# Loading a gated MLP's weights with four adjacent rows per partition instead of one

## The chip, the cores and the metric

One NeuronCore of a Trainium2 chip runs the kernel. The metric is device time in microseconds (us) of one execution; lower is better. The span that the profile of one execution shows is about 2 us shorter than the device time of that execution (62.4 and 64.23 us). Executions of one kernel here spread by about 1.5%. A run that is over 1.5% above the fastest of its kernel is called slow and left out of every ratio below; the others are the "fast" runs.

## The reference

```python
B, S, D, F = 32, 1, 1024, 3584          # all bfloat16
def reference(x, W_gate, W_up, W_down):
    gate = jnp.einsum("bsd,df->bsf", x, W_gate)      # 32x1024 @ 1024x3584
    up   = jnp.einsum("bsd,df->bsf", x, W_up)
    gate = gate * (gate > 0)                         # ReLU
    return jnp.einsum("bsf,fd->bsd", gate * up, W_down)   # 32x3584 @ 3584x1024
```

There are 32 rows of x and 22 MB of weights, each used once. That is a weight-streaming problem.

## The kernel before

All weight loads are issued by SP, ahead of everything, into SBUF that holds all three matrices. Each load has its own semaphore.

```python
Wg_sb = [P, KT, F];  Wu_sb = [P, KT, F];  Wd_sb = [P, NJT, D]      # P = 128, KT = 8, NJT = 28
for k in range(KT):                        # 16 transfers, each partition gets ONE row: 7168 bytes
    dma_list.append((("wg", k), Wg_sb[:, k, :], W_gate[k * P : (k + 1) * P, :]))
    dma_list.append((("wu", k), Wu_sb[:, k, :], W_up[k * P : (k + 1) * P, :]))
for n, gsz in enumerate([4, 4, 4, 4, 4, 4, 2, 1, 1]):   # 9 transfers, rows j*128 + p: 2048 bytes each
    dma_list.append((("wd", n), Wd_sb[:, j0:j1, :],
                     W_down[j0 * P : j1 * P, :].rearrange("(j p) d -> p j d", p=P)))
# ... cut ...
@block.sync
def _(sp):
    sp.dma_start(x_sb[:, :], x2).then_inc(sem_x, 16)
    for key, dst, src in dma_list:
        sp.dma_start(dst, src).then_inc(dma_sem[key], 16)
    issue_out_dmas(sp, "sp")               # output pieces go out on SP, ACT, POOL, SP
```

PE transposes x, then multiplies each weight tile as it lands, with x as the stationary operand, four 32-row results side by side in PSUM. ACT applies the ReLU, DVE multiplies by `up`, PE transposes the result (`h`), and W_down's tiles are multiplied as they land. The kernel waits for the last W_down tile, adds it, copies the sum out of PSUM and stores it in four pieces.

## Time and profile before

| | before |
|---|---|
| device time, median of 3 runs | 64.21 us (63.45 to 64.31) |
| span of the profiled execution | 62.4 us |
| PE busy | 25.6 us (41%) |
| HBM read | 22.09 MB, 355 GB/s over the whole span |

The page's slices of the span come first. Each column is a fortieth of the span (1.56 us). Digits are the busy share in tenths; "DMA" is the mean of the 16 DMA engines, "GB/s" what they moved.

```profile
PE   0202463265246326524632060293780533517800
...
DMA  0699999999999999999999999999999999993000
GB/s 0 180 400 405 414 423 423 428 432 428 423 418 428 418 418 418 428 414 423 414 418 424 414 410 381 386 389 386 385 390 385 389 386 386 389 385 139 11 20 22
```

The DMA row is 9 from the third slice to the thirty-sixth while PE is half idle: the stream of weights is the bound. The GB/s row has two plateaus, about 420 (gate and up) and about 387 (W_down). The windows view gives them exactly. Its columns are the window and its length, the busy time of each engine, the recorded PE clock, the DMA share and GB/s.

```profile
6.00:37.00 31.00, 14.51 (x98) 1.81 (x97) 0.00 (x0) 0.00 (x0) 0.00 (x0) 1.00 1.01 421
44.00:54.00 10.00, 4.80 (x76) 2.30 (x80) 0.69 (x1) 0.83 (x2) 0.00 (x0) 1.00 1.05 387
```

The chain that ended last, as the page sums it:

```profile
SPq L134 75%; DMA Wd_sb<-in_W_down_dram 16%; POOL out_dram L124 1%; PE O_ps L254 1%; ACT o_sb L168 1%; SPq L132 1%
```

"SPq L134" is the line that issues the weights. Its first twelve issues take 0.4 to 0.8 us each and later ones up to 9.2 us, while earlier transfers are still under way. What holds the later ones the trace does not show; with the DMA row at 9 throughout we count their time as the stream's. So read, 91% of the chain is the stream, and what follows it is short. The costliest group of the last stage, with its idle time, says the same from PE's side (7.7 us busy, 7.8 us idle before its instructions, of which W_down transfers ended 7.1):

```profile
L254 PE MATMUL O_ps<-Wd_sb,hT_sb 128*32 128x256 bf16 x112 | 7.7, 413 | 7.8 <-DMA Wd_sb<-in_W_down_dram 7.1
```

The trace also records every DMA packet and every semaphore increment. Each of these transfers raises its semaphore 16 times, and the page counts 16 DMA engines; the trace names no engine, and we read one landing as one engine. That fits the pace of gate and up: 128 packets of 7168 bytes are 8 for each engine, at 272 ns 2.18 us, and from the third transfer on their 8th landings come 2.17 to 2.20 us apart. These are the landings of four transfers, in us from the start of the span; "8th" is about the median engine:

```
before              8th     15th    16th
W_up, k=5          29.37   29.93   29.93
W_up, k=6          33.74   34.31   35.78
W_up, k=7          38.10   38.69   40.03
W_down, last piece 57.05   57.59   58.85
```

From 33.6 us on one engine is 1.2 to 1.5 us behind the fifteen others, and the last matmuls wait for it (they start at 58.90 us, the last landing is at 58.85). At 33.60 us the trace has a 16384-byte packet of the queue named "instruction", 1.07 us long; after that name we call it an instruction fetch.

### The profile page before, as it was taken

To read this page: it belongs to the slowest core of one execution; us is meant where nothing else is said; L and a number is where in the kernel's file an instruction comes from. 1 tells how busy PE (TensorE), PEld (TensorE's weight loads), DVE (VectorE), ACT (ScalarE), POOL (GpSimd) and SP (SyncE) were. 2 spreads that over 40 slices of the span, in tenths; PEclk is the share of its full clock that TensorE was granted. 3 is DMA by queue.
4 is the path that set the end of the run, shared out by engine and by line. 5 is a ranking of instruction groups with operands and counts; after the bars stand their busy time and mean duration, and the time that the engine had idled before them with its cause. 6 is when DMAs were issued, how large, how long until landed. Compare 5 with 4: busy or idle time off the path is not lost.

```text
span 62.4 us, 560 instructions
## 1 busy us (share of the span) xinstructions
PE 25.6 (41%) x240; PEld 6.6 (11%) x240; DVE 1.4 (2%) x2; ACT 4.2 (7%) x7; POOL 1.3 (2%) x7
## 2 busy tenths in 40 slices
PE   0202463265246326524632060293780533517800
PEld 0101000000000000000000000122340220303100
DVE  0000000000000000000000000013400000000000
ACT  5320000000000000000000000032430000000020
POOL 4000000000000000000000000000000000000030
DMA  0699999999999999999999999999999999993000
GB/s 0 180 400 405 414 423 423 428 432 428 423 418 428 418 418 418 428 414 423 414 418 424 414 410 381 386 389 386 385 390 385 389 386 386 389 385 139 11 20 22
DMA packets 6258, 22.19 MB, mean 356 GB/s; under 512 B 480, under 2 KB 592, under 8 KB 6256
## 3 DMA queue, kind: packets, MB, share of 16 engines
q1 hardware_dynamic: 6176, 22.12, 89.9%
q8 instruction: 2, 0.03, 0.2%
q10 hardware_dynamic: 48, 0.02, 0.1%
q0 software_dynamic: 32, 0.02, 0.1%
HBM read 22.09 MB, written 0.07 MB: 355 GB/s over the span
## 4 chain that ended last, share of the span: by engine, by line
SPq 75%; DMA 16%; issue 2%; POOL 1%; PE 1%; ACT 1%
SPq L134 75%; DMA Wd_sb<-in_W_down_dram 16%; POOL out_dram L124 1%; PE O_ps L254 1%; ACT o_sb L168 1%; SPq L132 1%
## 5 line engine op out<-in xcount | busy, mean ns | idle before, releaser
L201 PE MATMUL G_ps<-Wg_sb,xT_sb 128*32 128x512 bf16 x56 | 8.6, 618 | 13.0 <-DMA Wg_sb<-in_W_gate_dram 9.7
L201 PE MATMUL U_ps<-Wu_sb,xT_sb 128*32 128x512 bf16 x56 | 8.6, 621 | 9.5 <-DMA Wu_sb<-in_W_up_dram 9.5
L254 PE MATMUL O_ps<-Wd_sb,hT_sb 128*32 128x256 bf16 x112 | 7.7, 413 | 7.8 <-DMA Wd_sb<-in_W_down_dram 7.1
L254 PEld LDWEIGHTS O_ps<-Wd_sb,hT_sb 128*32 128x32 bf16 x112 | 3.2, 125 | 11.9 <-DMA Wd_sb<-in_W_down_dram 8.0
L159 ACT ACTIVATE g_sb<-G_ps 128x512 bf16<-128x512 f32 (+1 forms) x2 | 1.2, 596 | 37.8 <-PE U_ps L201 37.8
L201 PEld LDWEIGHTS G_ps<-Wg_sb,xT_sb 128*32 128x32 bf16 x56 | 1.3, 108 | 19.6 <-DMA Wg_sb<-in_W_gate_dram 12.3
L201 PEld LDWEIGHTS U_ps<-Wu_sb,xT_sb 128*32 128x32 bf16 x56 | 1.3, 109 | 16.1 <-DMA Wu_sb<-in_W_up_dram 15.9
L176 DVE TENSOR_TENSOR h_sb<-U_ps,g_sb 128x512 bf16<-128x512 f32 (+1 forms) x2 | 1.4, 690 | 43.7 <-ACT g_sb L159 43.7
L124 POOL DMA_DIRECT2D out_dram<-o_sb x1 | 0.6, 621 | 58.5 <-ACT o_sb L168 58.5
L188 PE MATMUL HTB_ps<-ident,x_sb 32*128 32x32 bf16 x8 | 0.4, 186 | 2.6 <-DMA x_sb<-in_x_dram 2.6
L155 ACT ACT_TABLE_LOAD x1 | 1.3, 1283 | 0.7 <-PEq L285 0.7
L168 ACT CAST o_sb<-O_ps 128x256 bf16<-128x256 f32 x1 | 0.4, 372 | 13.2 <-PE O_ps L254 13.2
L232 PE MATMUL HTA_ps<-ident,h_sb 128*128 128x128 bf16 x4 | 0.6, 308 | 0.6 <-DVE h_sb L176 0.6
L163 ACT COPY hT_sb<-HTA_ps 128x512 bf16<-128x512 bf16 x1 | 0.6, 586 | 1.4 <-PE HTA_ps L232 1.4
L232 PE MATMUL HTB_ps<-ident,h_sb 96*128 96x96 bf16 x4 | 0.5, 276 | 0.2 <-DVE h_sb L176 0.2
L163 ACT COPY hT_sb<-HTB_ps 128x384 bf16<-128x384 bf16 x1 | 0.5, 478 | 1.3 <-PE HTB_ps L232 1.3
L188 PEld LDWEIGHTS HTB_ps<-ident,x_sb 32*128 32x128 bf16 x8 | 0.3, 101 | 2.6 <-DMA x_sb<-in_x_dram 2.6
L232 PEld LDWEIGHTS HTA_ps<-ident,h_sb 128*128 128x128 bf16 x4 | 0.3, 130 | 1.5 <-DVE h_sb L176 1.5
L155 ACT COPY xT_sb<-HTB_ps 128x256 bf16<-128x256 bf16 x1 | 0.4, 372 | 1.0 <-PE HTB_ps L188 1.0
L232 PEld LDWEIGHTS HTB_ps<-ident,h_sb 96*128 96x128 bf16 x4 | 0.3, 127 | 0.7 <-DVE h_sb L176 0.7
L141 POOL TENSOR_SCALAR_AFFINE_SELECT ident<-ident 128x128 bf16<-128x128 bf16 x1 | 0.3, 287 | 0.2 <-POOL ident L139 0.2
L139 POOL MEMSET ident<- 128x128 bf16 x1 | 0.2, 204 | 0.3 <-POOLq L285 0.3
(4 smaller groups left out, 0.4 us busy)
## 6 DMA issues: line engine op xcount, KB each, us to landing
Wg_sb<-in_W_gate_dram SPq DMA_DIRECT2D x8, 896.0 KB, 16.1
Wu_sb<-in_W_up_dram SPq DMA_DIRECT2D x8, 896.0 KB, 17.8
Wd_sb<-in_W_down_dram SPq DMA_DIRECT2D x6, 1024.0 KB, 18.0
Wd_sb<-in_W_down_dram SPq DMA_DIRECT2D x1, 512.0 KB, 14.7
Wd_sb<-in_W_down_dram SPq DMA_DIRECT2D x2, 256.0 KB, 10.4
x_sb<-in_x_dram SPq DMA_DIRECT2D x1, 64.0 KB, 1.8
out_dram<-o_sb SPq DMA_DIRECT2D x2, 16.0 KB, 1.5
out_dram<-o_sb ACTq DMA_DIRECT2D x1, 16.0 KB, 1.6
```

Of the source, the lines that this page charges most:

```text
L124: eng.dma_start(dst, src).then_inc(sem_out[i], 16)
L132: sp.dma_start(x_sb[:, :], x2).then_inc(sem_x, 16)
L134: sp.dma_start(dst, src).then_inc(dma_sem[key], 16)
L155: act.copy(out=xT_sb[:, :], in_=xT_ps).then_inc(sem_xT_sb, 1)
L159: act.activation(out=g_sb[g][0:np_, :], in_=G_ps[g][0:np_, :], func=ACT.Relu).then_inc(sem_g, 1)
L163: act.copy(out=hT_sb[g][:, :, 0:np_], in_=HT_ps[g].rearrange("p (t q) -> p t q", t=TPC)[:, :, 0:np_],).then_inc(sem_hT_sb, 1)
L168: act.copy(out=o_sb[:, :], in_=O_ps[:, 0:DQ]).then_inc(sem_o, 1)
L176: dve.tensor_tensor(out=h_sb[g][0:np_, :], in0=U_ps[g][0:np_, :], in1=g_sb[g][0:np_, :], op=ALU.mult,).then_inc(sem_h, 1)
L188: ins = pe.transpose(xT_ps[:, k * NB : (k + 1) * NB], x_sb[:, k * P : (k + 1) * P], ident[0:NB, 0:NB],)
L201: return pe.matmul(ps[q * NB : (q + 1) * NB, :], lhsT=xT_sb[:, k * NB : (k + 1) * NB], rhs=w[:, k, c * FC : (c + 1) * FC], start=(k == 0), ...
L232: ins = pe.transpose(HT_ps[g][:, t * P : t * P + np_], h_sb[g][0:np_, t * P : (t + 1) * P], ident[0:np_, 0:np_],)
L254: ins = pe.matmul(O_ps[q * NB : (q + 1) * NB, 0:DQ], lhsT=hT_sb[g][:, t, qq * NB : (qq + 1) * NB], rhs=Wd_sb[:, j, q * DQ : (q + 1) * DQ], ...
```

## The change

The intent: give each partition several rows that are adjacent in HBM and adjacent in SBUF, so that a DMA packet is longer. The row order inside a contraction is free, provided that x (or h) is transposed in the same order; so the transposes read every fourth column. The waits become coarser: 4 gate/up transfers instead of 16. POOL issues no output piece any more: the third piece moves from POOL to SP and the fourth from SP to ACT. The core of the diff:

```diff
-WD_GROUPS = os.environ.get("GLU_WDG", "4,4,4,4,4,4,2,1,1")
+BLOCKS = [4, 4]  # rows per partition of each gate/up transfer
-        out_queues = ["sp", "act", "pool", "sp"]
+        out_queues = ["sp", "act", "sp", "act"]
-        for k in range(KT):
-            dma_list.append((("wg", k), Wg_sb[:, k, :], W_gate[k * P : (k + 1) * P, :]))
-            dma_list.append((("wu", k), Wu_sb[:, k, :], W_up[k * P : (k + 1) * P, :]))
+        for k2 in range(NK2):                      # k0 = first row block, R = 4
+            rows = slice(k0 * P, (k0 + R) * P)
+            cols = slice(k0 * F, (k0 + R) * F)
+            dma_list.append(
+                (("wg", k2), Wg_sb[:, cols], W_gate[rows, :].rearrange("(p r) f -> p (r f)", r=R)))
+            ...  # the same for W_up
-                    W_down[j0 * P : j1 * P, :].rearrange("(j p) d -> p j d", p=P),
+                dma_list.append((("wd", c), Wd_sb[:, c, :], blk.rearrange("(p r) d -> p (r d)", r=RD)))
+            ...  # the last block in pieces of 2, 1 and 1 rows
-                    x_sb[:, k * P : (k + 1) * P],
+                        x_sb[:, P * k0 + r : P * (k0 + R) : R],
-                        h_sb[g][0:np_, t * P : (t + 1) * P],
+                        h_sb[g][0:np_, r:FC:RD],
-            for j in range(0, TPC): down(j)
-            transposes(1)
+                if i == 2:                          # the second transposes after 2 row tiles, not 4
+                    transposes(1)
```

## The prediction

> **What bounds the kernel.** The weight stream, nothing else. In the page's slices all 16 DMA engines are 90% busy or more from about 3 to 55 us of a 62.4 us span, while PE is busy 41%. The chain of waits is 75% the weight-issuing line [...], 16% the last W_down transfer, then 0.43 us of PE, 0.38 us of ACT and the output.
>
> **Where the stream loses time.** From the trace's DMA packets: a 7168-byte packet takes 272 ns (median), a 2048-byte packet 84 ns. Two points give a line: 9 ns fixed per packet plus 27.3 B/ns. That is 421 GB/s in the gate/up stage (windows view) and 386 GB/s in the W_down stage. [...]
>
> **What the change does.** The same 22 MB, laid out so that a partition reads 4 adjacent rows: packets of 28672 B for gate/up (4 transfers, not 16) and 8192 B for W_down (tail 4096, 2048, 2048). Estimates from the line above, per engine:
> - gate/up: 128 x 272 = 34.8 us becomes 32 x 1060 = 33.9 us: -0.9 us.
> - W_down: 224 x 84.3 = 18.9 us becomes 48 x 309 + 8 x (159 + 84 + 84) = 17.5 us: -1.4 us.
> - The fourth output piece moves from POOL to a second ACT issue. Now the POOL one lands last, at 61.84 us; the second SP one at 61.64. Gain about 0.2 us.
>
> All three lie on the critical path: -2.5 us in sum.
>
> **What it costs.** Coarser waits: PE starts on gate/up only when 3.67 MB has landed (about 10.5 us, before 5.8), and after the last W_up transfer it has 3 more rows of W_up (21 matmuls at about 0.15 us) before the last row. So the first hT comes near 46 us instead of 43.9. PE works off a W_down chunk in 1.05 us and one arrives each 2.5 us, so it is caught up before 52 us: off the path.
>
> **What stays.** At 33.6 us a 16 KB instruction fetch (1.07 us, queue "instruction") rides on one DMA engine; from then on the 16th landing of each weight transfer is about 1.3 us after the 15th (57.59 and 58.85 us for the last). The PE program is as long, so I expect this to remain, merely later (about 39 to 42 us, in the W_down stage).
>
> **Prediction:** 61.7 us, range 60.8 to 62.9. Faster by over 2%: 0.80, within 2%: 0.17, slower: 0.03.
>
> **What would show it.** Gate/up packets about 1060 ns and 430 GB/s; W_down packets about 310 ns and 425 GB/s or more; last weight landing near 56.4 us instead of 58.85; last output landing about 2.8 us after that; still one straggling engine.
>
> **What would make it wrong.** Packets of 28 KB are outside the sizes seen here: if they are split or run no faster, 0.9 us is gone. [...] If the instruction fetch falls on an engine that is early in the 0.8 us skew of landings, up to 0.8 us more is won; if the second fetch (57.5 us now, when most engines were done) meets the stream, or the last small packets share its engine, up to 1 us is lost.

## The result, and the profile after

| | before | after |
|---|---|---|
| device time, median | 64.05 us (15 runs) | 61.9 us (12 runs, 61.51 to 62.29) |
| ratio after/before | | 0.967, 95% interval 0.963 to 0.971 |
| span of the profiled execution | 62.4 us | 59.9 us |
| last weight landing | 58.85 us | 56.49 us |

A ratio here is the mean time of one kernel's fast runs over that of the other's fast runs of the same rounds, so it is not quite the ratio of the medians quoted beside it. The change is 3.3% faster, and the result is correct.

The windows view of the kernel after, same stretches as before:

```profile
6.00:37.00 31.00, 9.96 (x77) 3.09 (x77) 0.00 (x0) 0.00 (x0) 0.00 (x0) 0.73 1.00 430
44.00:54.00 10.00, 3.84 (x77) 2.09 (x77) 0.68 (x1) 0.48 (x1) 0.00 (x0) 0.66 1.01 413
```

421 has become 430 GB/s and 387 has become 413. The page's slices show PE in bursts; the single GB/s columns swing from 306 to 555 because a packet's bytes are counted in the slice in which it starts and a packet of 28672 bytes is 1.06 us long, two thirds of a slice:

```profile
PE   0200000079600199200493000796246424518800
...
DMA  0977998979799897998979898999999999994001
GB/s 0 331 325 306 498 421 364 555 344 536 344 440 478 344 555 325 498 421 364 555 325 536 364 421 344 437 426 405 410 432 410 437 426 410 402 392 168 11 19 25
```

The chain of waits is still the stream and the short tail; the POOL output is gone from it:

```profile
DMA Wd_sb<-in_W_down_dram 49%; SPq L137 43%; PE O_ps L262 1%; ACT o_sb L173 1%; SPq L135 1%
```

The group that multiplies W_down still waits for DMA (5.9 of 6.6 us), so PE did catch up after its late start. The last rows of the timeline (start, length, engine, line, what) show the tail after the last landing at 56.49 us: four matmuls, the copy, and the output issues, now two on each of two queues.

```profile
L262 PE MATMUL O_ps<-Wd_sb,hT_sb 128*32 128x256 bf16 x112 | 6.4, 353 | 6.6 <-DMA Wd_sb<-in_W_down_dram 5.9
```

```profile
56.54 0.40 PE L262 MATMUL O_ps<-Wd_sb,hT_sb 128*32 128x256 bf16 x4 [0.23 <-DMA Wd_sb<-in_W_down_dram]
57.00 0.37 ACT L173 CAST o_sb<-O_ps 128x256 bf16<-128x256 f32 x1 [11.38 <-PE O_ps L262]
57.39 0.81 SPq L127 DMA_DIRECT2D out_dram<-o_sb  x2
57.40 0.86 ACTq L127 DMA_DIRECT2D out_dram<-o_sb  x2
```

The landings split the 2.4 us of span into terms (all from the two profiled executions, us; each row is the stretch between two of the times):

| stretch | before | after | difference | predicted |
|---|---|---|---|---|
| to the 8th landing of the last gate/up transfer | 38.10 | 37.49 | -0.61 | -0.9 |
| from there to the 8th landing of the last W_down piece | 18.95 (to 57.05) | 17.52 (to 55.01) | -1.43 | -1.4 |
| from there to the 16th landing of that piece (the delayed engine) | 1.80 (to 58.85) | 1.48 (to 56.49) | -0.32 | 0 |
| from there to the end of the span | 3.53 (to 62.38) | 3.44 (to 59.93) | -0.09 | -0.2 |
| sum | 62.38 | 59.93 | -2.45 | -2.5 |

### The profile page after: what moved, and what is told of

It reads as the page before. It is cut to its first block, busy times and chain, and to the rows that moved or that the text cites. A ratio compares the mean times of both kernels' runs of the same rounds, so it can differ in the third digit from the quotient of the medians.

```text
span 59.9 us, 547 instructions
## 1 busy us (share of the span) xinstructions
PE 21.1 (35%) x240; PEld 8.0 (13%) x240; DVE 1.4 (2%) x2; ACT 4.2 (7%) x7; POOL 0.7 (1%) x6
## 4 chain that ended last, share of the span: by engine, by line
DMA 49%; SPq 44%; issue 1%; PE 1%; ACT 1%
DMA Wd_sb<-in_W_down_dram 49%; SPq L137 43%; PE O_ps L262 1%; ACT o_sb L173 1%; SPq L135 1%
## 5 line engine op out<-in xcount | busy, mean ns | idle before, releaser
L210 PE MATMUL G_ps<-Wg_sb,xT_sb 128*32 128x512 bf16 x56 | 7.8, 605 | 14.3 <-DMA Wg_sb<-in_W_gate_dram 14.3
L210 PE MATMUL U_ps<-Wu_sb,xT_sb 128*32 128x512 bf16 x56 | 7.1, 603 | 10.5 <-DMA Wu_sb<-in_W_up_dram 10.5
L262 PE MATMUL O_ps<-Wd_sb,hT_sb 128*32 128x256 bf16 x112 | 6.4, 353 | 6.6 <-DMA Wd_sb<-in_W_down_dram 5.9
L210 PEld LDWEIGHTS G_ps<-Wg_sb,xT_sb 128*32 128x32 bf16 x56 | 2.4, 132 | 18.3 <-issue 12.3
L210 PEld LDWEIGHTS U_ps<-Wu_sb,xT_sb 128*32 128x32 bf16 x56 | 2.1, 133 | 15.4 <-DMA Wu_sb<-in_W_up_dram 12.4
```

The costliest lines, as they stand in the source:

```text
L210: return pe.matmul(ps[q * NB : (q + 1) * NB, :], lhsT=xT_sb[:, k, :], rhs=w[:, k * F + c * FC : k * F + (c + 1) * FC], start=(k == 0), sto ...
L262: ins = pe.matmul(O_ps[q * NB : (q + 1) * NB, 0:DQ], lhsT=hT_sb[g][:, r, qq * NB : (qq + 1) * NB], rhs=Wd_sb[:, c, r * D + q * DQ : r * D ...
```

## The experiments

The theory: a packet has a fixed cost (9 ns by the line of the prediction), the stream is the critical path, so longer packets shorten the kernel; and the engine that lands last is delayed by an instruction fetch. The rivals: the number of transfers, the order of HBM addresses, or the output queue make the gain; the lag has another cause. Every run was correct. Each is compared with runs of the kernel before on the same chip in the same rounds, except two.

### One part at a time: e1, e2, e3

e1 keeps the new gate/up layout and restores the old W_down layout and output queues:

```diff
-blk.rearrange("(p r) d -> p (r d)", r=RD)      # W_down, 8192-byte packets
+blk.rearrange("(r p) d -> p r d", r=RD)        # 2048-byte packets, rows 256 KB apart
-h_sb[g][0:np_, r:FC:RD]
+h_sb[g][0:np_, r * P : (r + 1) * P]
-out_queues = ["sp", "act", "sp", "act"]
+out_queues = ["sp", "act", "pool", "sp"]
```

> Gate/up in 28672-byte packets (4 transfers), W_down as before in 2048-byte packets with its rows 256 KB apart, outputs as before. Packet theory (9 ns fixed per packet): gate/up stage at about 432 GB/s, W_down stage still 386 GB/s, time 0.9 us under before, ratio about 0.986. Rival, that the slow W_down stage is what counts and the gate/up stage was at its ceiling of about 421 GB/s: no change, ratio 1.00.

e2 keeps the new W_down layout alone:

```diff
-BLOCKS = [4, 4]
+BLOCKS = [1] * 8
-out_queues = ["sp", "act", "sp", "act"]
+out_queues = ["sp", "act", "pool", "sp"]
```

> W_down in 8192-byte packets, gate/up as before (16 transfers of 7168-byte packets), outputs as before. Packet theory: W_down stage goes from 386 to about 422 GB/s, gate/up stays 421, time 1.4 us under before, ratio about 0.978. Rival, that the second HBM-side limit near 386 GB/s holds in that stage whatever the packets: ratio 1.00.

e3 is the kernel before with the new output queues alone:

```diff
-out_queues = ["sp", "act", "pool", "sp"]
+out_queues = ["sp", "act", "sp", "act"]
```

> The kernel before with the third output piece sent by ACT rather than POOL. By the landings (61.84 us for POOL's, 61.64 for the second of SP) 0.2 us less[...]: ratio 0.994 to 0.997. Rival: no difference, 1.00.

| run | median us | ratio to before | 95% interval | expected |
|---|---|---|---|---|
| e1, gate/up only | 63.86 | 0.995 | 0.986 to 1.003 | 0.986 |
| e2, W_down only | 62.87 | 0.980 | 0.972 to 0.988 | 0.978 |
| e3, outputs only | 63.87 | 0.999 | 0.991 to 1.006 | 0.994 to 0.997 |
| product of the three | | 0.973 | | |
| the change | 61.9 | 0.967 | 0.963 to 0.971 | |

W_down gives most of the gain, as costed. The output's 0.1 to 0.2 us can't be told from zero by time. The windows of e2 show its gate/up stage as in before and its W_down stage faster (417 GB/s; 422 was expected, 386 by the rival):

```profile
6.00:37.00 31.00, 14.58 (x98) 1.92 (x98) 0.00 (x0) 0.00 (x0) 0.00 (x0) 1.00 1.02 421
44.00:54.00 10.00, 5.66 (x84) 2.66 (x84) 0.69 (x1) 0.96 (x2) 0.00 (x0) 1.00 1.01 417
```

e1 gave less than expected, though its interval just reaches 0.986; by its time alone it can't be told from no gain. Its windows show that both stages run at the rates that the theory says (430 and 388 GB/s), but that the passage from one to the other does not. The windows of e1 (gate/up, the passage, W_down), then the passage in before and in after:

```profile
6.00:37.00 31.00, 9.95 (x77) 3.10 (x77) 0.00 (x0) 0.00 (x0) 0.00 (x0) 0.73 1.00 430
37.50:40.50 3.00, 2.37 (x23) 0.92 (x26) 0.00 (x0) 0.00 (x0) 0.00 (x0) 0.50 1.02 369
44.00:54.00 10.00, 5.08 (x80) 2.55 (x84) 0.69 (x1) 1.37 (x3) 0.00 (x0) 0.50 1.05 388
```

```profile
37.50:40.50 3.00, 0.34 (x4) 0.17 (x8) 0.00 (x0) 0.00 (x0) 0.00 (x0) 1.00 1.03 386
```

```profile
37.50:40.50 3.00, 2.69 (x26) 1.07 (x29) 0.00 (x0) 0.00 (x0) 0.00 (x0) 0.51 1.02 431
```

In e1 the 8th landings of the first two 1 MB W_down transfers come 3.08 and 2.85 us after the one ahead of them, against 2.72 and 2.71 in before. While some engines still moved packets of 28672 bytes and others already had packets of 2048, the latter took 130 ns on average (37 to 38 us), against 88 in e1's own W_down stage (44 to 54 us). That is about 0.5 us given back at a border that the change itself does not have (its first W_down transfer takes 2.48 us, like the next ones). It is one profile, and it says where the time went, not by which mechanism. What it shows for the method: a one-part experiment can create a border that neither kernel has, so its parts need not add up. (The times don't prove that they don't: each part is known to about 0.8% only.)

### Same transfers, same addresses, short packets: e5

64 unused bytes after each row in SBUF stop the rows from being adjacent there. Everything else is as in the change.

```diff
-Wg_sb = [P, KT * F];  Wd_sb = [P, NFC, RD * D]
+PAD = 32  # unused elements after each row in SBUF
+Wg_sb = [P, KT, F + PAD];  Wd_sb = [P, NFC * RD, D + PAD]
-Wg_sb[:, cols],              W_gate[rows, :].rearrange("(p r) f -> p (r f)", r=R)
+Wg_sb[:, k0 : k0 + R, 0:F],  W_gate[rows, :].rearrange("(p r) f -> p r f", r=R)
```

> The changed kernel with 64 unused bytes after each weight row in SBUF: same 13 transfers, same HBM addresses in the same order, same outputs, but rows no longer adjacent in SBUF, so packets of 7168 and 2048 bytes again. Packet theory: gate/up back to 421 GB/s, W_down back to 386 GB/s, time as before less the output's part, ratio 0.995 to 1.00. Rival 1 (fewer transfers) and rival 2 (each engine walks adjacent HBM addresses instead of rows 256 KB apart): still as fast as the change, 0.967.

Measured: 63.48 us, ratio 0.990 (0.984 to 0.996). The trace counts the packets of before again, 7168 and 2048 bytes. So most of the gain goes when the packets are short, with the same 13 transfers and the same addresses. But probably not all of it goes: 0.995 or more was expected, which the interval just reaches. The windows of e5:

```profile
6.00:37.00 31.00, 9.95 (x77) 3.06 (x77) 0.00 (x0) 0.00 (x0) 0.00 (x0) 0.87 1.01 425
44.00:54.00 10.00, 5.38 (x88) 2.99 (x88) 0.69 (x1) 1.56 (x3) 0.00 (x0) 0.60 1.05 398
```

The mean of five 8th-landing intervals of the 1 MB W_down transfers separates the two causes: 2.71 us in before, 2.63 us in e5 (same packet size, but in adjacent rows, where before stepped 256 KB from packet to packet), 2.49 us in the change. Times 7 MB: about 0.6 us of the W_down gain comes with the order of the addresses (or with the padding in SBUF, which no run separates from it) and about 1.0 us with the longer packets. Gate/up divides in the same way: at the pace between landings the stage takes 35.0 us in before, 34.6 in e5 (four transfers for sixteen, adjacent rows, still 7168-byte packets) and 34.0 in the change, so about 0.4 us of the 1.0 us comes without longer packets. The prediction had put all of it on the packets.

### Many transfers, long packets: e6 and e9

e6 cuts each gate/up transfer of the change into four of 32 adjacent partitions:

```diff
-sp.dma_start(dst, src).then_inc(dma_sem[key], 16)
+for i in range(0, P, P // 4):
+    sp.dma_start(dst[i : i + P // 4, :], src[i : i + P // 4, :]).then_inc(dma_sem[key], 16)
-pe.wait_ge(dma_sem[("wg", k2)], 16)
+pe.wait_ge(dma_sem[("wg", k2)], 16 * 4)
```

> The changed kernel with each gate/up transfer cut into 4 of 32 partitions: 16 gate/up transfers as in before, but each of 28672-byte packets. Packet theory: gate/up packets 1062 ns, time as after the change, ratio 0.967. Rival (fewer transfers make the gain in that stage): the gate/up part is lost, ratio about 0.98.

Measured: 97.42 us, ratio 1.521. Neither theory had that. The windows of e6, its gate/up stage and its W_down stage:

```profile
6.00:70.00 64.00, 9.95 (x77) 3.10 (x77) 0.00 (x0) 0.00 (x0) 0.00 (x0) 1.00 1.01 211
78.00:90.00 12.00, 5.78 (x99) 3.12 (x100) 1.38 (x2) 1.61 (x4) 0.00 (x0) 0.66 1.01 413
```

The gate/up stage runs at half rate (211 GB/s, against 430 in the change) although all DMA engines count as busy (share 1.01); the W_down stage, untouched, runs at the change's rate (413). Two things differ from the change: the number of transfers, and that each takes 32 adjacent partitions instead of all 128. The HBM side is no likely rival: each transfer of e6 reads one contiguous block of 0.9 MB, as each gate/up transfer of before does at 421 GB/s. e9 tells the two apart by the same 16 transfers with every fourth partition:

```diff
-for i in range(0, P, P // 4):
-    sp.dma_start(dst[i : i + P // 4, :], src[i : i + P // 4, :])...
+for i in range(4):
+    sp.dma_start(dst[i:P:4, :], src[i:P:4, :])...
```

> As e6 (16 gate/up transfers of 28672-byte packets), but each transfer takes every fourth partition instead of 32 adjacent ones. If e6 was slow [...], this one [...] runs at full rate: gate/up packets 1062 ns, ratio 0.967 as the change. If many transfers, or two packets per engine and transfer, were what cost e6 its time, this one is as slow as e6 (97 us). If it is near 0.98, the number of transfers carries part of the change's gain.

Measured: 62.09 us, ratio 0.970 (0.957 to 0.982); its gate/up window shows the full rate:

```profile
6.00:37.00 31.00, 9.95 (x77) 3.06 (x77) 0.00 (x0) 0.00 (x0) 0.00 (x0) 0.72 1.00 429
```

So the choice of partitions, not the number of transfers, cost e6 its time (211 against 429 GB/s); by which mechanism, no run shows. And 16 gate/up transfers with long packets run as fast as 4: 429 against 430 GB/s. The time alone would not settle that, since its interval holds the rival's 0.98; the rate does. The rival "fewer transfers" falls.

### The delayed engine: e7, e4 and e11

e7 puts 64 dummy matmuls (128 PE instructions: the page counts a weight load for each matmul, 240 and 240 in the change) into PE's idle time before the first weights:

```diff
             pe.wait_ge(sem_xT_sb, 1)
+            for _ in range(64):
+                pe.matmul(D_ps[0:32, 0:32], lhsT=ident[:, 0:32], rhs=ident[:, 0:32], start=True, stop=True)
```

> The changed kernel with 64 dummy matmuls (128 PE instructions) into an unused PSUM bank, in PE's idle time before the first weights. Theory, that the engine which lands last from mid-stream on is delayed by PE's instruction fetch: the two 16 KB fetches (41.4 and 55.1 us in the changed kernel) come some 128 instructions earlier, near 15 us and near 46 to 49 us, and the 1.2 us lag of one landing starts with the first of them. If both ride on the same DMA engine the lag grows to about 2.4 us and the time by about 1.2 us (ratio about 0.985); if on two engines, the lag stays about 1.2 us and the ratio 0.967. Rival, that the lag has another cause: its onset stays near 42 us whatever the fetches do.

Measured: 61.89 us, ratio 0.966 (0.959 to 0.972). From the traces:

```
                          after             e7
instruction fetches at    41.39, 55.14      16.07, 50.58 us
W_gate 1st     15th,16th  12.16, 12.28      12.31, 12.52
W_up 1st       15th,16th  20.68, 20.75      20.99, 22.22
W_down c=1     15th,16th  42.74, 44.00      42.97, 44.21
W_down c=4     15th,16th  50.18, 51.45      50.42, 51.66
W_down c=5     15th,16th  52.67, 53.95      53.83, 54.19
W_down last    15th,16th  55.26, 56.49      56.35, 56.68
```

The onset of the lag moved with the first fetch, from the transfer that lands after 41.4 us to the first that lands after 16.1. The second fetch, which came after nearly all engines were done in the change, now falls into the stream and delays a second engine by about 0.9 us, at the transfer that lands after 50.6. The time does not change, because the delays are on two engines and the end waits for the worse one (last landing 56.68 us, in the change 56.49). The first fetch in the change is one packet of 1.10 us. It is not hidden from this stream (DMA share 1.01 from 44 to 54 us): in each W_down transfer that lands after it, one landing is 1.23 to 1.28 us behind the fifteenth.

e4 (the change) and e11 (e7) ask which engine it is. Fifteen tiny transfers of k = 1 to 15 partitions follow the last weights on the same queue. As no trace names an engine, we number them from 0 by the first tiny transfer in which they take part: number 11 is the one that joins at k = 12.

```diff
+            for k in range(1, 16):
+                sp.dma_start(diag_sb[0:k, k * 256 : (k + 1) * 256], x2[0:k, 0:256]).then_inc(sem_diag[k], 16)
```

> The changed kernel, with 15 tiny transfers of k partitions (k = 1 to 15) behind the last weight transfer on the same queue. If the last one to land is always the same delayed engine[...] then the landing time as a function of k jumps by about 1 us at one k: that engine is number k-1. If it never jumps, the delayed engine is number 15 (or the tiny transfers do not share its queue). The weights' last landing should stay about 1.2 us after the 15th.

> The kernel of e7 (fetches near 16 and 50 us) with the 15 tiny transfers of e4 behind the stream. If an instruction fetch always rides on the same DMA engine, the jump in the landing times is at k = 12 (engine 11) again for the first fetch. If the engine differs from page to page or run to run, the jump is at another k, and sparing fixed engines as in e8 can't work in general. The second delayed engine, if any, shows as another jump.

Both: 62.04 and 61.82 us. They were run at other times. The expected jump was not there: each tiny transfer costs an engine 0.17 to 0.22 us, so the engines that joined first, which take part in all the later ones, pile up delay and are last (k=2 lands last at 55.94 us in e4, k=15 at 58.24). What answers is the one landing in each transfer that has none 0.17 to 0.22 us before it in the transfer ahead: that engine takes part for the first time. In e4 the delayed engine's last weight landing is 56.86 us, and a new landing 0.17 us later, 57.03, appears at k=12. In e11 the two delayed engines' are 56.63 and 56.44, and new landings at 56.80 and 56.59 appear at k=12 and k=13. The way that the landings build up allows the count: up to k=13 each transfer has the landings of the one before and exactly one new one. By it the first fetch rode on engine 11 in both runs, at 42 and at 17 us, and the second on engine 12 in the one run where it could be told.

### Sparing the delayed engine: e8

The last piece goes as two transfers, of 121 and of 7 partitions. The author expected the first to use 11 engines and the second 7, so that engines 11 to 15 have nothing of the last piece to move:

```diff
+                if key == ("wdp", 3):
+                    sp.dma_start(dst[0:121, :], src[0:121, :]).then_inc(dma_sem[key], 16)
+                    sp.dma_start(dst[121:P, :], src[121:P, :]).then_inc(dma_sem[key], 16)
-                    pe.wait_ge(dma_sem[key], 16)
+                    pe.wait_ge(dma_sem[key], 32 if key == ("wdp", 3) else 16)
```

> The changed kernel; the last W_down piece (2048 bytes for each of 128 partitions) goes as two transfers of 121 and 7 partitions, which [...] use only the first 11 DMA engines; the delayed one was number 11 there, the first that is spared. If the delayed engine is number 11 or higher again, its last landing comes 0.67 us sooner, the others' about 0.3 us later: last weight landing near 56.0 us instead of 56.5, 0.3 to 0.65 us gained on the change, ratio to before about 0.958. If it is another engine (0 to 10) now, the last landing is 0.3 us later, ratio about 0.972.

Measured: 62.04 us, ratio 0.967 (0.962 to 0.973): the same as the change. The split did what it should: the last piece's semaphore has 18 landings from engines (11 and 7 are 18), the last of them at 56.15 us, and the delayed engine is not among them. But the timeline shows PE waiting longer for the piece before:

```profile
53.95 1.04 PE L267 MATMUL O_ps<-Wd_sb,hT_sb 128*32 128x256 bf16 x16 [1.34 <-DMA Wd_sb<-in_W_down_dram]
...
55.92 1.23 PE L267 MATMUL O_ps<-Wd_sb,hT_sb 128*32 128x256 bf16 x16 [0.93 <-DMA Wd_sb<-in_W_down_dram]
```

In the change those matmuls start at 54.00 and 55.25. The two-row piece's last landing came at 55.88 us in e8 (55.21 in the change), the one-row piece after it at 56.49. In the change the delayed engine's last 2048-byte packets took 84 ns each; in e8 the eight of the one-row piece follow one another without a gap on the one engine still busy at the end, from 54.90 us, and six of them took 120 to 192 ns. They end 0.49 us later than in the change (55.99, 55.50), and the landing follows after 0.50 us instead of 0.36. So the 0.67 us of work taken off that engine was lost again to slower packets and later landings. Two causes come to mind: the transfer of 121 partitions, which runs beside these packets (in e6 a choice of partitions cost half the rate, 211 against 429 GB/s in e9), and the second fetch, 55.11 to 56.24 us. The trace speaks for the first: the 2048-byte packets of all engines that start from 54.0 to 54.6 us already took about 110 ns (median; 87 in the change), over 0.5 us before that fetch begins. How that transfer would slow them was not tested.

### The start of the stream: e10 and e12

e10 issues x from ACT, so that SP's first instruction is a weight transfer:

```diff
-            sp.dma_start(x_sb[:, :], x2).then_inc(sem_x, 16)
+            act.dma_start(x_sb[:, :], x2).then_inc(sem_x, 16)      # on ACT, before its first wait
```

> The changed kernel with the load of x issued by ACT instead of ahead of the weights on SP. In the changed kernel x is issued at 0.74 us and the first weights at 1.16 us, so the weight stream, which is the critical path, should start and end 0.4 us sooner: last weight landing near 56.1 us, 0.4 us less, ratio to before about 0.961. If the first weights' start is set by something other than the issue order, no change: 0.967.

e12 is e10 with shorter packets first:

```diff
-BLOCKS = [4, 4]
+BLOCKS = [1, 3, 4]
```

> The kernel of e10 (x issued by ACT) with the first gate/up transfers of 1 and 3 rows per partition instead of 4, so that the first packets are 7168 bytes. In before the first 7168-byte packets took 0.37 to 0.83 us and the 8th landing of the first transfer came 0.4 us later than a full-rate start would give; with 28672-byte first packets they took 1.4 to 2.1 us and it came 0.8 us later. Theory, that large first packets lose the start: the stream ends 0.35 us or more sooner than in e10, ratio to before about 0.960. Rival, that the start-up loss does not hang on the first packets' size: 0.967 as e10.

Measured: e10 61.76 us, ratio 0.967 (0.958 to 0.976); e12 62.24 us, ratio 0.970 (0.962 to 0.978). Both are the rivals' numbers. In e10 the first weight packet did start sooner (1.77 us, 2.23 in the change), but the 8th landing of the first transfer came at 12.06 us against 11.98 (x's packets now fall among the weights', at 3.6 to 4.2 us). In e12 the median engine's last weight landing came at 55.52 us, against 55.13 in e10. So neither an earlier first issue nor smaller first packets brought the stream to its full rate sooner. What holds it back was not found.

No run beat the change beyond the noise: e7 (0.966) and e10 (0.967) equal it, so the change is the version to keep.

## Why the prediction was right

The predicted 61.7 us was measured as 61.9, inside the range of 60.8 to 62.9, and "faster by over 2%" was right. Point by point:

- *The weight stream bounds the kernel.* Right. The chain of waits is the stream in both profiles, and PE's coarser waits did not matter: the first W_down matmuls started at 43.52 us, not "near 46", because the last W_up landing came at 37.77 us, ahead of the fetch and not after it, and the 29 matmuls from there to the first ReLU took 3.2 us (0.11 us each, not 0.15). PE's first gate matmul came at 12.42 us, not "about 10.5".
- *28672-byte packets take 1060 ns, 8192-byte packets 309 to 310 ns.* Right: medians of 1062 and 311 ns. A line through two packet sizes of the kernel before was good for four times the larger. One figure behind the line needs care: the median record of a 2048-byte packet in before is 88 ns, not 84. The records overlap (DMA share 1.05 in that window), and 84 is the spacing of the packets: 2.71 us for a transfer that gives each engine 32 of them is 84.7 ns. The spacing is what adds up to the stream's time.
- *Gate/up: -0.9 us.* The size was off. Between transfers it is right: four at 8.50 us against sixteen at 2.19 us is 34.0 against 35.0. But the start was later: the 8th landing of the first transfer minus one such interval is 3.48 us in the change and 3.07 in before. The stretch gave -0.61 us. The estimate had taken the start as equal. In e12 smaller first packets did not mend it.
- *W_down: -1.4 us.* Right in sum (-1.43), incomplete in its reason: e5 shows that about a third of it comes without longer packets. The forecast rate of "425 GB/s or more" was missed: 413 in the window, or 422 by the 2.49 us that a transfer of 1 MB takes.
- *Output: -0.2 us.* Not seen: the last output landed 2.98 us after the last weights (59.47 and 56.49), in before 2.99 (61.84 and 58.85), because the second piece of ACT now lands last, as POOL's did before. The span shows -0.09; e3 could not tell it from zero.
- *One straggling engine stays, "merely later (about 39 to 42 us)".* Right: the fetch came at 41.39 us and the 16th landing lagged the 15th by 1.23 us at the end. e7 shows the cause by moving it. How far the delayed engine is behind the median differs between profiles (1.80 us before, 1.48 after), which we put down to where that engine stood before the fetch, when the landings were already spread by 0.8 us in before and 0.6 in the change; this 0.32 us made up for what gate/up lacked. The close agreement of the sums is thus partly luck.

## What to carry to other kernels

Where the weight stream is the critical path, lay out rows so that what one partition reads in a transfer is contiguous on both sides, and estimate the gain from two packet sizes in the trace: t = a + bytes/rate held here from 2 KB to 28 KB (9 ns and 27.3 B/ns, from 84 and 272 ns, gave 1060 ns; measured 1062), with t the spacing of packets; part of a came with the order of the addresses or the padding (about 0.6 us of the W_down gain, e5). Mind which partitions a transfer covers: blocks of 32 adjacent ones gave 211 GB/s in the gate/up stage (e6), all 128 gave 430 and every fourth 429 (e9), where 16 transfers instead of 4 cost nothing measurable. At the end of a DMA-bound kernel compare the 15th with the 16th landing: one engine that has carried an instruction fetch held up the last matmuls here by 1.26 us before the change and 1.23 us after it.

## Further measurements

- Each fetch in the stream took about 1 us of one DMA engine (1.07 us in before, 1.10 in the change) and put that engine about 0.9 to 1.3 us behind the others until the end (e7, e11). By the count above, the two fetches of e11 took engines 11 and 12.
- The size of a packet decided at an unchanged number of transfers: W_down 398 GB/s with 2048-byte packets (e5) and 413 with 8192; gate/up 425 with 7168 (e5) and 430 with 28672. 16 gate/up transfers of 0.9 MB ran at 429 GB/s (e9).
- 2048-byte packets whose HBM addresses step by 256 KB ran at 387 GB/s (before), against 398 in adjacent rows (e5, which also has the padding in SBUF).
- The start is slow: in the change the first sixteen 28672-byte packets took 1.2 to 2.1 us, against 1.06 later. Where long and short packets meet, the rate was 369 GB/s for 3 us in e1.
- Transfers of 32 adjacent partitions ran at 211 GB/s (e6), transfers of the same size that step through the partitions at 429 (e9).
- The profile's PE clock needs care: the windows of before list 1.00 throughout, though its rounds of three or four gate/up matmuls start 0.43 us apart (40.54, 40.97, 41.40), which is the spacing that the profile of after has where it lists 0.50 (38.22, 38.65, 39.07), and twice the spacing where it lists 0.96 (40.61, 40.83, 41.04, in the window from 40 to 45 us).
